# Three raw weight buffers against one converted one in a recurrence feeding two feed-forward layers

## The chip, the cores and the metric

The kernel runs on one core of one Trainium2 chip. The metric is the device time of one execution in microseconds; the median of three runs before the change is 770.36 us (769.48 to 771.55).

## The reference

Four batches of eight heads, 768 steps and a head size of 48 go through a gated linear recurrence; its output, 3072 tokens of 384, goes through two feed-forward layers (hidden sizes 2048 and 1024).

```python
for t in range(S):                                   # per batch and head, state is 48 x 48
    cur = einsum('bhd,bhe->bhde', u * kt, vt)
    y[:, :, t] = einsum('bhd,bhde->bhe', rt, state + cur)
    state = wt[..., None] * state + einsum('bhd,bhe->bhde', kt, vt)
...
h = x @ w_in;  x = (h - tanh(h)) @ w_out             # layer 1
...
h = x @ w_in2; e = exp(h - max(h)); h = h * e / (sum(e) + 1e-9)
x = (h - mean(h)) / sqrt(var(h) + 1e-6) * g_ln @ w_out2   # layer 2
```

The two pairs of weight matrices come as 64-bit floats, which the kernel reads as pairs of 32-bit words; all else is 32-bit.

## The kernel before, in words

**Units and blocks.** The recurrence is cut into 24 units of 128 steps (NU), all heads of a unit together. Four units give one block of 512 tokens (UB = 4, NB = 6 blocks). A unit goes through `att_pre` and `att_0` to `att_4`: transposes of w, r and k, a cumulative product of w by a scan (line 285), its logarithm and exponential on ScalarE (288, 289), products with r and k, score matmuls (312), a masked copy (314), transposes of k (318) that ScalarE copies to `kn` (319), the state update (328 to 340), and the output matmuls (354), which leave the tokens in `xs`. Units 0 to 7 (below TURN = 8) are loaded by `att_load` and transposed by TensorE; later ones by `load_turned` and VectorE.

**Layer 1.** A loop over s runs 96 steps, 16 a block. Step s does `part1` (nine matmuls into `hp`, line 401; a polynomial for h - tanh(h) with scratch tiles t, q and y; a split of the result into a rounded part and a rest, g) and `part2` of two steps before (nine matmuls into three accumulators `x2p`, line 425). At a block's end ScalarE copies the accumulators to `x2o` tiles (line 430), which borrow the tags q, t and y, and SyncE stores them (431). In the first and the last block (`ends`) the polynomial's middle term goes into `hp`, elsewhere into q.

**Weights.** Each of the 16 slices of layer 1's weights is loaded as raw 64-bit words into a tile `raw` (pool cvr, lines 364 to 387: four DMAs of 96 KB and one of 384 KB), converted by `convert` and written to the resident tile `wa`. The conversion is one ScalarE operation on the low words (121), three VectorE operations on each half (129, 130, 131, the last into `cv_x` of pool cv), a rounding copy on ScalarE (134) and a subtraction on GpSimd (135) that reads `cv_x` again. Both pools have two buffers. Slices 0 and 1 are loaded early; slice s+2 is loaded and converted in step s of the first block. Layer 2's eight slices are converted the same way in the last block (`conv_b`, into `wb`), with one pass over the whole tile and a scale (133).

**Flags.** Everything the fast path assumes is collected in a column per test of the tile `flags`: w within bounds for each unit (`check_w`, line 241: two ScalarE Relu passes, each followed by a read of the accumulator), the size of h, and the smallness of the weights' values (`check_pair`, lines 140 and 141, which re-loads a raw pair in the blocks after the first). For units 0 to 7 `check_w` stands in `att_pre` ahead of GpSimd's product (254), and its junk output goes to a q tile, or to the tile that 254 writes next.

**Order.** SyncE's queue issues all loads and stores in one order and waits at an instruction whose buffer is not free. The framework orders each engine's instructions ahead of time by priority (the order of the program's lines) and by its own estimate of when operands are ready; each engine then runs its list in order. Layer 2 (lines 463 to 568) follows the loop.

The lines the prediction speaks of, in short:

```python
cv = pool(L, "cv", 2); cvr = pool(L, "cvr", 2)              # 603, 604
v.tensor_tensor(x[:, s], a, L_[:, s], ALU.add)              # 131
nc.scalar.copy(hi, xf)                                      # 134
nc.gpsimd.tensor_tensor(lo, xf, hi, ALU.subtract)           # 135
q = self.gp.tile([128, BLK], F32, tag="q", name="q")        # 403
```

Of the kernel before, what the change touches and what calls it, by code (L numbers as in the profile page):

```python
# [8 lines left out]
F32 = mybir.dt.float32  # L9
F32R = mybir.dt.float32r  # L10
U32 = mybir.dt.uint32
I32 = mybir.dt.int32
U8 = mybir.dt.uint8
# [19 lines left out]
ROW = 4 * 4 * D  # L33
TURN = 2 * UB


W_LO, W_HI = 0.75, 1.34

# [20 lines left out]
class Kern:  # L59
# [7 lines left out]
    def setup(self, const):  # L67
        nc = self.nc
        self.ident = const.tile([128, 128], F32, name="ident")
        self.zeros = const.tile([128, 1], F32, name="zeros")  # L70
        self.ub = const.tile([128, H, D], F32, name="ub")
        self.mask = const.tile([128, 4, 128], U8, name="mask")
        self.cst = const.tile([128, 8], F32, name="cst")
        self.nflag = 2 * NU + NB * NM + NM + NM2
        self.flags = const.tile([128, self.nflag], F32, name="flags")
        make_identity(nc, self.ident)
        nc.vector.memset(self.zeros, 0.0)
        for i, val in enumerate((F_SB, -F_T2, W_LO, -W_HI, -0.5, P_SB, P_MIN, FLAG_MIN2)):
            nc.vector.memset(self.cst[:, i:i + 1], val)
        (self.c_fsb, self.c_t2, self.c_lo, self.c_hi, self.c_mhalf, self.c_sb, self.c_min,  # L80
         self.c_flag) = (self.cst[:, i:i + 1] for i in range(8))

    def setup_mask(self, ones):
        nc = self.nc
        nc.gpsimd.memset(ones, 1.0)
        nc.gpsimd.affine_select(
            out=ones, in_=ones, compare_op=ALU.is_gt, fill=0.0, base=0,
            pattern=[[0, 4], [1, 128]], channel_multiplier=-1,
        )
        nc.vector.tensor_copy(self.mask, ones)  # L90

# [20 lines left out]
    def convert(self, pool, raw, hi, lo, scale=None, bank=None):  # L112
# [10 lines left out]
        for i in range(n):  # L123
            s = slice(i * 2 * DM // n, (i + 1) * 2 * DM // n)
            if bank is None:
                a = x
            else:
                a = bank.tile([128, 4, C], F32, tag="a", name="cv_a").rearrange("p j t -> p (j t)")[:, 0:DM].bitcast(U32)
            v.tensor_scalar(a, H_[:, s], 3, 0x3FFFFFF8, ALU.logical_shift_left, ALU.bitwise_and)
            v.scalar_tensor_tensor(a, H_[:, s], 0xC0000000, a, ALU.bitwise_and, ALU.bitwise_or)  # L130
            v.tensor_tensor(x[:, s], a, L_[:, s], ALU.add)  # L131
        if scale is not None:
# [10 lines left out]
    def check_pair(self, rpool, n):  # L143

        raw = self.load_pair(rpool, n)
        with self.tc.issue_after(self.last_act.ins):
            self.check(raw, 2 * NU + NB * NM + n)

# [90 lines left out]
    def check_w(self, u, w, tmp):  # L239
        for i, (b, s) in enumerate(((self.c_lo, -1.0), (self.c_hi, 1.0))):  # L240
            self.nc.scalar.activation(tmp, w, AF.Relu, bias=b, scale=s,
                                      accum_out=self.flags[:, 2 * u + i:2 * u + i + 1])

    def att_pre(self, u):
        nc = self.nc
        t = self.rk(u)
        r, k = (t[:, 0, :, 0:D], t[:, 1, :, 0:D]) if u < TURN else (self.nat[:, 0], self.nat[:, 1])
        ruk = self.ruk
        if u <= UB:
            ruk = self.gp.tile([128, BLK], F32, tag="y", name="ruk")[:, 0:DM].rearrange("p (h d) -> p h d", h=H)  # L250
        if u < TURN:
            w = self.gp.tile([128, BLK], F32, tag="q", name="cw")[:, 0:DM].rearrange("p (h d) -> p h d", h=H) if u < UB else ruk
            self.check_w(u, t[:, 2, :, 0:D], w)
        nc.gpsimd.tensor_tensor(ruk, r, self.ub, ALU.mult)
        nc.gpsimd.tensor_tensor(ruk, k, ruk, ALU.mult)
        nc.vector.reduce_sum(self.dg[u % 2].rearrange("p e j -> p j e"), ruk.rearrange("p (j e) d -> p j e d", e=2), axis=AX)
# [44 lines left out]
    def att_2(self, u):  # L301
# [11 lines left out]
        for e in range(2):  # L313
            v.copy_predicated(self.aq[:, e], self.mask, ps[e])
        if u % NC < NC - 1:
# [79 lines left out]
    def part1(self, i, m):  # L395
# [6 lines left out]
        t = self.gp.tile([128, BLK], F32, tag="t", name="t")  # L402
        q = self.gp.tile([128, BLK], F32, tag="q", name="q")
        y = self.gp.tile([128, BLK], F32, tag="y", name="y")
# [5 lines left out]
        nc.scalar.activation(p, t, AF.Square, bias=self.c_fsb, scale=F_S)  # L410
        col = 2 * NU + i * NM + m
        self.last_dve = v.scalar_tensor_tensor(y, p, F_E, y, ALU.add, ALU.mult)  # L412
# [8 lines left out]
    def part2(self, i, m, gs):  # L421
# [5 lines left out]
        if m == NM - 1:  # L427
            for d in range(KM):
                o = self.gp.tile([128, BLK], F32, tag="qty"[d], name="x2o")
                self.nc.scalar.activation(o, self.x2p[d], AF.Copy, scale=-1.0)  # L430
# [162 lines left out]
def fast_path(tc, K, const):  # L593
# [8 lines left out]
    L, R, R2 = ExitStack(), ExitStack(), ExitStack()  # L602
    cv = pool(L, "cv", 2)
    cvr = pool(L, "cvr", 2)
    K.gp = pool(L, "gp", 2)
# [33 lines left out]
    for s in range(-2, NB * NM + 2):  # L639
# [37 lines left out]
        n, due = divmod(3 * (s - NM), 7)  # L677
        if 0 <= n < NM + NM2 and due < 3:
            K.check_pair(cvr, n)
# [219 lines left out]
```

## Time and profile before

| what | value |
|---|---|
| median of 3 runs | 770.36 us (769.48 to 771.55) |
| the profiled execution's own time | 775.22 us |
| its span in the trace | 773.4 us |
| busy in the span: PE, DVE, ACT, POOL | 725.0, 585.2, 490.8, 419.0 us |
| mean granted TensorE clock | 0.982 of full speed |
| DMA: moved, mean rate, share of 16 engines | 110.80 MB, 143 GB/s, 52.9% |

PE is TensorE, DVE VectorE, ACT ScalarE, POOL GpSimd, SPq the queue of SyncE that issues the transfers. Lines are numbered as in the kernel above. An engine runs its instructions in order, so a wait at one of them holds up all that stand behind it; a row of waits gives the total, the number and the longest.

### The profile page before, as it was taken

The numbers are of one execution on the slowest core, as the hardware profiler recorded it, in microseconds if no ns is written. First come the engines' busy times: TensorE is split into PE (matmuls) and PEld (weight loads), VectorE is DVE, ScalarE is ACT, GpSimd is POOL, SyncE is SP. The second block draws the span as 40 slices with busy tenths as digits, with TensorE's granted clock in tenths as the row PEclk, the third lists the DMA queues.
The fourth block names the chain that finished last, engine by engine and source line by source line (L and its number), as shares of the span: only waits on it lengthen the run. The fifth ranks groups of instructions, "written<-read, shape, count | busy, mean of one in ns | idle before, by whom it ended". The sixth has DMA issues, their size and how long they took to land.

```text
span 773.4 us, 13992 instructions
## 1 busy us (share of the span) xinstructions
PE 725.0 (94%) x4882; PEld 599.2 (77%) x4882; DVE 585.2 (76%) x999; ACT 490.8 (63%) x920; POOL 419.0 (54%) x397
## 2 busy tenths in 40 slices
PE   6558988999999999999999999999989999999986
PEld 4446667778877888887888887878769989989976
DVE  4868888877766687677677774487669999999992
ACT  4436777588676877686768665787745555554552
POOL 7424575666566666556655654467525454454440
PEclk9879999999999999999999999999999999999999
DMA  9962666666756756576555510232045555555631
GB/s 156 189 127 69 157 185 151 147 169 179 175 146 162 196 143 174 133 205 177 138 154 168 155 62 11 82 123 83 10 158 183 168 178 172 175 169 168 188 104 46
DMA packets 171632, 110.80 MB, mean 143 GB/s; under 512 B 93600, under 2 KB 160288, under 8 KB 171552
## 3 DMA queue, kind: packets, MB, share of 16 engines
q1 hardware_dynamic: 171552, 109.82, 52.9%
q8 instruction: 40, 0.66, 0.4%
q14 instruction: 40, 0.33, 0.1%
HBM read 88.81 MB, written 20.97 MB: 142 GB/s over the span
## 4 chain that ended last, share of the span: by engine, by line
PE 49%; DVE 28%; ACT 10%; DMA 5%; SPq 4%; issue 3%; POOL 1%; ACTq 0%; DVEq 0%; POOLq 0%
PE hp L401 19%; PE x2p L425 19%; DVE tw L539 6%; DVE so L514 4%; PE y L354 4%; DVE e L508 4%; DMA raw<-in_moe_w_out_dram 3%; ACT e L515 3%; DVE part L504 3%; PE qk L312 3%; SPq L367 2%; PE o L564 2%; DVE cv_x L131 2%; SPq L201 1%; PE kt L318 1%
## 5 line engine op out<-in xcount | busy, mean ns | idle before, releaser
L425 PE MATMUL x2p<-g,wa 128*128 128x512 f32 x864 | 226.0, 400 | 9.6 <-ACT g L415 7.9
L401 PE MATMUL hp<-xs,wa 128*128 128x512 f32 x864 | 216.0, 395 | 2.5 <-POOL wa L135 1.3
L425 PEld LDWEIGHTS x2p<-g,wa 128*128 128x128 f32 x864 | 158.7, 189 | 49.6 <-ACT g L415 9.9
L401 PEld LDWEIGHTS hp<-xs,wa 128*128 128x128 f32 x864 | 163.4, 190 | 39.7 <-POOL wa L135 2.3
L418 POOL TENSOR_TENSOR g<-y,g 128x512 fp32r<-128x512 f32 x96 | 129.6, 1351 | 48.4 <-ACT g L415 39.0
L407 DVE TENSOR_TENSOR y<-hp,t 128x512 f32<-128x512 f32 x96 | 65.8, 686 | 76.8 <-ACT t L406 60.4
L564 PE MATMUL o<-wb,ts 128*128 128x384 f32 x576 | 105.1, 336 | 2.5 <-POOL ts L543 2.5
L482 PE MATMUL h<-wb,x2s 128*128 128x512 f32 x432 | 104.1, 392 | 3.2 <-POOL x2s L471 1.7
L413 ACT ACTIVATE q<-t,cst 128x512 f32<-128x512 f32 x96 | 69.5, 724 | 55.7 <-DVE y L412 55.1
L564 PEld LDWEIGHTS o<-wb,ts 128*128 128x128 f32 x576 | 100.7, 188 | 4.8 <-POOL ts L543 3.2
L482 PEld LDWEIGHTS h<-wb,x2s 128*128 128x128 f32 x432 | 80.4, 188 | 20.7 <-POOL x2s L471 2.7
L417 POOL TENSOR_SCALAR g<-y 128x512 fp32r<-128x512 f32 x64 | 40.3, 630 | 81.5 <-DVE y L412 77.4
L406 ACT ACTIVATE t<-hp 128x512 f32<-128x512 f32 x96 | 56.5, 588 | 27.2 <-PE hp L401 26.3
L515 ACT ACTIVATE e<-so 128x1024 f32<-128x1024 f32 x24 | 25.5, 1061 | 59.6 <-DVE so L514 59.6
L543 POOL TENSOR_TENSOR ts<-tw,ts 128x512 fp32r<-128x512 f32 x44 | 55.9, 1292 | 4.4 <-ACT ts L542 4.4
L412 DVE SCALAR_TENSOR_TENSOR y<-q,y 128x512 f32<-128x512 f32 x64 | 51.4, 803 | 2.9
L471 POOL TENSOR_TENSOR x2s<-x2s 128x384 fp32r<-128x384 f32 x24 | 24.4, 1017 | 48.1 <-ACT x2s L470 43.7
L297 POOL TENSOR_TENSOR inv<-inc,kh 112x512 f32<-112x512 f32 x24 | 29.1, 1213 | 37.4 <-ACT kh L289 33.7
L410 ACT ACTIVATE q<-t,cst 128x512 f32<-128x512 f32 x64 | 46.3, 723 | 1.3
L539 DVE STREAM_TRANSPOSE tw<-sw 128x1024 f32<-128x1024 f32 x22 | 44.5, 2022 | 0.4 <-issue 0.3
L517 POOL TENSOR_TENSOR st<-st,cst 128x1 f32<-128x1 f32 x23 | 12.6, 549 | 53.0 <-DVE st L498 45.3
L121 ACT ACTIVATE raw<-raw 128x768 uint32<-128x768 uint32 x24 | 21.8, 908 | 27.9 <-DMA raw<-in_moe_w_out_dram 24.3
(138 smaller groups left out, 1182.4 us busy)
## 6 DMA issues: line engine op xcount, KB each, us to landing
raw<-in_moe_w_out_dram SPq DMA_DIRECT2D x48, 384.0 KB, 4.0
raw<-in_moe_w_in_dram SPq DMA_DIRECT2D x128, 96.0 KB, 2.8
dso<-so SPq DMA_DIRECT2D x22, 512.0 KB, 3.0
sw<-dso SPq DMA_DIRECT2D x88, 128.0 KB, 3.0
rkw<-in_k_dram SPq DMA_DIRECT2D x64, 96.0 KB, 2.7
rkw<-in_r_dram SPq DMA_DIRECT2D x64, 96.0 KB, 2.4
rkw<-in_w_dram SPq DMA_DIRECT2D x64, 96.0 KB, 2.4
raw<-in_moe_w_in_dram SPq DMA_DIRECT2D x16, 384.0 KB, 3.2
```

The costliest lines, as they stand in the source:

```text
L401: self.mm(hp, self.wa[:, a, m, j * 128:(j + 1) * 128], xs[:, b, j], start=n == 0, stop=n == len(seq) - 1)
L406: nc.scalar.activation(t, hp, AF.Square)
L407: v.tensor_tensor(y, hp, t, ALU.mult)
L412: self.last_dve = v.scalar_tensor_tensor(y, p, F_E, y, ALU.add, ALU.mult)
L413: self.last_act = nc.scalar.activation(q, t, AF.Relu, bias=self.c_t2, accum_out=self.flags[:, col:col + 1])
L418: g.tensor_tensor(gs[:, 1], y, gs[:, 0], ALU.subtract)
L425: self.mm(self.x2p[d], self.wa[:, a, m, sl], gs[:, b], start=m == 0 and n == 0, stop=m == NM - 1 and n == 2)
L482: self.mm(p[:, f], xs[:, a, j], w, start=q == 0, stop=q == 8)
L515: nc.scalar.activation(e, so, AF.Square, accum_out=va)
L539: self.turned = nc.vector.transpose(x.rearrange("p k (t b) -> p b k t", b=4), sw)
L543: nc.gpsimd.tensor_tensor(ts[:, 1, k], x[:, k], ts[:, 0, k], ALU.subtract)
L564: self.mm(p, ts[:, a, k], self.wb[:, b, k, DM:], start=q == 0, stop=q == 3 * NM2 - 1)
```

## The change

`cvr`, the pool of raw words, gets three buffers and `cv`, the pool of converted words, one. For layer 2 the last VectorE step of the conversion writes over the raw high words (every second word of the tile), which ScalarE and GpSimd then read; for layer 1 it still writes `cv_x`. The q tag gets one buffer. The mask becomes one 128x128 tile broadcast over four heads. The bounds of w are tested by one Square of (w - 1.045) and one Relu of its excess over 0.087025, with one accumulator read in place of two. For units 0 to 7 `check_w` goes out of `att_pre`; in its stead two more turns of `check_pair` (n = 24 and 25, in steps 72 and 75, the fifth block) re-load the w of four units each into a raw tile by four DMAs and test the 128x1536 values in two passes.

```diff
-        self.mask = const.tile([128, 4, 128], U8, name="mask")
+        self.mask = const.tile([128, 128], U8, name="mask")
...
-        nc.vector.tensor_copy(self.mask, ones)
+        nc.vector.tensor_copy(self.mask, ones[:, 0])
...
-            v.tensor_tensor(x[:, s], a, L_[:, s], ALU.add)
+            v.tensor_tensor(H_ if bank is None else x[:, s], a, L_[:, s], ALU.add)
+        if bank is None:
+            xf = H_.bitcast(F32)
...
-        raw = self.load_pair(rpool, n)
+        if n < NM + NM2:
+            raw = self.load_pair(rpool, n)
+            with self.tc.issue_after(self.last_act.ins):
+                self.check(raw, NW + NB * NM + n)
+            return
+        h = n - NM - NM2
+        raw = rpool.tile([128, 2, DM, 2], U32, tag="raw", name="raw").rearrange("p i f two -> p (i f two)").bitcast(F32)
+        w = raw.rearrange("p (i h d) -> p i h d", i=UB, h=H)
+        for i in range(UB):
+            b, c = divmod(UB * h + i, NC)
+            self.nc.sync.dma_start(out=w[:, i], in_=self.w[b, :, c * C:(c + 1) * C, :].rearrange("h p d -> p h d"))
         with self.tc.issue_after(self.last_act.ins):
-            self.check(raw, 2 * NU + NB * NM + n)
+            self.nc.scalar.activation(raw, raw, AF.Square, bias=self.c_mid)
+            self.nc.scalar.activation(raw, raw, AF.Relu, bias=self.c_rad, accum_out=self.flags[:, h:h + 1])
...
-        for i, (b, s) in enumerate(((self.c_lo, -1.0), (self.c_hi, 1.0))):
-            self.nc.scalar.activation(tmp, w, AF.Relu, bias=b, scale=s,
-                                      accum_out=self.flags[:, 2 * u + i:2 * u + i + 1])
+        self.nc.scalar.activation(tmp, w, AF.Square, bias=self.c_mid)
+        self.nc.scalar.activation(tmp, tmp, AF.Relu, bias=self.c_rad, accum_out=self.flags[:, u + NW - NU:u + NW - NU + 1])
...
-        if u < TURN:
-            w = self.gp.tile([128, BLK], F32, tag="q", name="cw")[:, 0:DM].rearrange("p (h d) -> p h d", h=H) if u < UB else ruk
-            self.check_w(u, t[:, 2, :, 0:D], w)
...
-            v.copy_predicated(self.aq[:, e], self.mask, ps[e])
+            v.copy_predicated(self.aq[:, e], self.mask.unsqueeze(1).to_broadcast([128, 4, C]), ps[e])
...
-        q = self.gp.tile([128, BLK], F32, tag="q", name="q")
+        q = self.gp.tile([128, BLK], F32, tag="q", name="q", bufs=1)
...
-                o = self.gp.tile([128, BLK], F32, tag="qty"[d], name="x2o")
+                o = self.gp.tile([128, BLK], F32, tag="qty"[d], name="x2o", bufs=1 if d == 0 else 2)
...
-    cv = pool(L, "cv", 2)
-    cvr = pool(L, "cvr", 2)
+    cv = pool(L, "cv", 1)
+    cvr = pool(L, "cvr", 3)
...
-        if 0 <= n < NM + NM2 and due < 3:
+        if 0 <= n < NM + NM2 + TURN // UB and due < 3:
```

## Rows read from the trace of the kernel before

**Rows 1.** Busy time by stretch: PE, PEld, DVE, ACT, POOL, granted clock, DMA share, GB/s

```profile
26.00:56.00 30.00, 18.57 (x278) 14.91 (x278) 21.61 (x47) 11.89 (x20) 10.39 (x9) 0.72 0.83 152
56.00:150.00 94.00, 81.88 (x597) 63.38 (x597) 81.59 (x155) 63.93 (x118) 56.00 (x42) 0.95 0.57 143
150.00:470.00 320.00, 318.19 (x2426) 255.93 (x2428) 228.49 (x401) 231.44 (x463) 192.98 (x186) 1.00 0.58 155
```

**Rows 2.** Chain of waits, by line, in 56 to 150 us

```profile
by line: DMA raw<-in_moe_w_out_dram 20.5%; PE hp L401 13.2%; PE x2p L425 8.2%; SPq L367 8.1%; DVE st L340 6.3%; issue 5.0%; PE qk L312 3.9%; ACT g L415 3.1%; ACT raw L121 2.8%; POOL g L418 2.8%; DVE y L407 2.7%; DVE cv_a L129 2.7%; PE y L35
```

**Rows 3.** ScalarE's waits for raw words, 56 to 150 us: total, times, longest

```profile
ACT raw L121 <- DMA raw<-in_moe_w_out_dram: 12.3, 7, 3.4
ACT raw L121 <- DMA raw<-in_moe_w_in_dram: 2.7, 1, 2.7
```

**Rows 4.** SyncE's own queue, its longest waiter in 20 to 150 us

```profile
SPq L367 <- DVE cv_x L131: 41.7, 11, 10.1
```

**Rows 5.** Chain of waits in 18 to 66 us, four pieces: start, us, what

```profile
31.88 0.72 ACT ruk L241 x2
...
32.62 0.71 ACT ruk L241 x2
...
37.19 5.21 DMA raw<-in_moe_w_out_dram
...
43.38 0.43 ACT kn L319
```

**Rows 6.** Timeline of TensorE: transposes that kn copies; busy time in 37 to 43 us

```profile
35.90 1.01 PE L318 MATMUL x2p<-ident,kh 112*128 112x112 f32 x4
...
37.00:43.00 6.00, 0.00 (x0) 0.00 (x0) 2.46 (x5) 1.32 (x2) 4.13 (x4) 0.50 1.09 215
```

**Rows 7.** Timeline of ScalarE: first and last of the 13 rounding copies of slices 2 to 14

```profile
66.90 0.82 ACT L134 CAST wa<-cv_x 128x768 fp32r<-128x768 f32 x1
...
147.12 0.82 ACT L134 CAST wa<-cv_x 128x768 fp32r<-128x768 f32 x1
```

**Rows 8.** Timelines, two conversions from the first write of cv_x to its last read

```profile
78.50 0.54 DVE L131 CUSTOM_DVE_ANT_0 cv_x<-raw,cv_a 128x768 uint16<-128x768 uint16 x1
...
83.39 1.84 POOL L135 TENSOR_TENSOR wa<-cv_x,wa 128x768 fp32r<-128x768 f32 x1
...
115.75 0.54 DVE L131 CUSTOM_DVE_ANT_0 cv_x<-raw,cv_a 128x768 uint16<-128x768 uint16 x1
...
117.86 0.55 DVE L131 CUSTOM_DVE_ANT_0 cv_x<-raw,cv_a 128x768 uint16<-128x768 uint16 x1
...
120.21 0.82 ACT L134 CAST wa<-cv_x 128x768 fp32r<-128x768 f32 x1
...
121.11 1.86 POOL L135 TENSOR_TENSOR wa<-cv_x,wa 128x768 fp32r<-128x768 f32 x1 [0.98 <-ACT wa L134]
```

**Rows 9.** Timeline of ScalarE at the end of the fourth block; the store's time to landing

```profile
415.29 0.59 ACT L430 ACTIVATE x2o<-x2p 128x512 f32<-128x512 f32 x1
...
416.80 0.72 ACT L413 ACTIVATE q<-t,cst 128x512 f32<-128x512 f32 x1 [0.25 <-DVE y L412]
...
422.24 0.71 ACT L410 ACTIVATE q<-t,cst 128x512 f32<-128x512 f32 x1
...
423.48 0.72 ACT L410 ACTIVATE q<-t,cst 128x512 f32<-128x512 f32 x1
...
424.20 0.72 ACT L413 ACTIVATE q<-t,cst 128x512 f32<-128x512 f32 x1
...
x2d<-x2o SPq DMA_DIRECT2D x18, 256.0 KB, 2.4
```

**Rows 10.** Groups of the two kinds of tests, by shape; busy time in 440 to 480 us

```profile
L141 ACT ACTIVATE raw<-raw,cst 128x768 f32<-128x768 f32 x24 | 23.9, 994 | 0.3
...
L241 ACT ACTIVATE cw<-rkw,cst 128x384 f32<-128x384 f32 x8 | 4.9, 616 | 4.7 <-DMA rkw<-in_w_dram 4.6
...
440.00:480.00 40.00, 40.00 (x308) 32.12 (x307) 24.19 (x42) 24.04 (x48) 22.48 (x23) 1.00 0.18 53
```

**Rows 11.** Groups, by shape: GpSimd's subtraction for layer 2

```profile
L135 POOL TENSOR_TENSOR wb<-cv_x,wb 128x768 fp32r<-128x768 f32 x8 | 17.0, 2119 | 3.0 <-PE x2p L425 3.0
```

More of the change, by code (lines that the diff above doesn't have):

```diff
@@ L34 @@
 TURN = 2 * UB
-W_LO, W_HI = 0.75, 1.34
+NW = NU - TURN + TURN // UB
+W_MID, W_RAD2 = 1.045, 0.087025
 P_MIN = 1e-30
@@ L69, in setup @@
         self.ident = const.tile([128, 128], F32, name="ident")
-        self.zeros = const.tile([128, 1], F32, name="zeros")
         self.ub = const.tile([128, H, D], F32, name="ub")
-        self.mask = const.tile([128, 4, 128], U8, name="mask")
+        self.mask = const.tile([128, 128], U8, name="mask")
         self.cst = const.tile([128, 8], F32, name="cst")
-        self.nflag = 2 * NU + NB * NM + NM + NM2
-        self.flags = const.tile([128, self.nflag], F32, name="flags")
+        self.nflag = NW + NB * NM + NM + NM2
+        flags = const.tile([128, self.nflag + 1], F32, name="flags")
+        self.flags, self.zeros = flags[:, 0:self.nflag], flags[:, self.nflag:]
         make_identity(nc, self.ident)
         nc.vector.memset(self.zeros, 0.0)
-        for i, val in enumerate((F_SB, -F_T2, W_LO, -W_HI, -0.5, P_SB, P_MIN, FLAG_MIN2)):
+        for i, val in enumerate((F_SB, -F_T2, -W_MID, -W_RAD2, -0.5, P_SB, P_MIN, FLAG_MIN2)):
             nc.vector.memset(self.cst[:, i:i + 1], val)
-        (self.c_fsb, self.c_t2, self.c_lo, self.c_hi, self.c_mhalf, self.c_sb, self.c_min,
+        (self.c_fsb, self.c_t2, self.c_mid, self.c_rad, self.c_mhalf, self.c_sb, self.c_min,
          self.c_flag) = (self.cst[:, i:i + 1] for i in range(8))
@@ L410, in part1 @@
         nc.scalar.activation(p, t, AF.Square, bias=self.c_fsb, scale=F_S)
-        col = 2 * NU + i * NM + m
+        col = NW + i * NM + m
         self.last_dve = v.scalar_tensor_tensor(y, p, F_E, y, ALU.add, ALU.mult)
```

## The prediction

> **What bounds the kernel now.** I read the busy times by stretch first, to find where TensorE is not the bound. From 150 to 470 us it is: 318.19 of 320 us busy at clock 1.00 [rows 1]. Nothing this change does to another engine there can shorten the time, short of a new stall. The stretches with slack are 26 to 56 us (18.57 of 30 us busy, clock 0.72) and 56 to 150 us (81.88 of 94, clock 0.95) [rows 1]. Whatever these two lose, all later work starts earlier by as much, so the change is priced in them.
>
> Then the chain of waits. From 56 to 150 us its largest entry is not an engine: the transfers of raw weights hold 20.5% of 94 us, 19.3 us, and SyncE's issue of them another 8.1%, 7.6 us [rows 2]. Why are they late? The queue's own waits say: SyncE stood 41.7 us, in 11 waits, before a raw load because VectorE's line 131 had not yet given a raw buffer back [rows 4]; and ScalarE, which has the first operation on the words, sat idle 12.3 + 2.7 = 15.0 us for them [rows 3]. So in the first block two raw buffers are too few: a load starts when the last conversion is over, and the next conversion waits for it. The rounding copies of slices 2 to 14 start at 66.90 and 147.12 us, 12 spacings of 6.69 us [rows 7]; a step of the first block takes that long.
>
> The start differs. On its chain stand unit 4's test of w (0.72 + 0.71 us) and 5.21 us of slice 2's raw transfer, after which ScalarE gets to `kn` of unit 2 at 43.38 [rows 5]. Its transposes were over at 36.91 [rows 6]: it stood behind the raw operation in ScalarE's list. TensorE did nothing from 37 to 43 us [rows 6]. But there the DMA engines have no room: share 1.09, 215 GB/s [rows 6].
>
> **The change part by part.** (1) *Test of w out of the early units.* Each unit loses two passes and two accumulator reads. On the chain stands only unit 4's pair, 1.43 us [rows 5]; the rest ran beside other work. What is late next is the logarithm behind it, which needs a VectorE scan ending at almost the same time, so I take 0.5 of a possible 1.4 us. GpSimd's product of unit 4, which waited for the test's junk, now waits for its r transfer alone.
>
> (2) *Third raw buffer, at the start.* Slice 2's load needs no buffer back and can be issued ahead of the loads of units 4 and 5. If so, `kn` of unit 2 moves from 43.38 to about 37.4, right behind its transposes: 6.0 us at most [rows 5, 6]. If the queue keeps its order, nothing: the DMA engines are full, and an earlier raw load only pushes the units' loads back. No row decides between them; I take the middle, 3 us, and keep 0 and 6 as ends.
>
> (3) *Third raw buffer, in the first block.* Load m then waits for the conversion three before, about 6.7 us sooner than now, against waits of 3.4 us at most [rows 3]: ScalarE's 15.0 us of waiting go. What is late next is either VectorE or the single `cv_x`. VectorE is busy 81.59 of 94 us [rows 1], so 0.868 of a spacing, 5.8 us: that floor allows 12 x (6.69 - 5.8) = 10.7 us.
>
> (4) *One buffer of converted words.* This adds a wait: line 131 of the next slice must follow GpSimd's line 135 of this one. The loop from the first write to the last read takes 78.50 to 85.23, 6.73 us, in one conversion and 115.75 to 122.97, 7.22 us, in another [rows 8]: mean 6.98, longer than the spacing now. Of it 0.54 + 0.55 + 0.82 + 1.86 = 3.77 us is work [rows 8] and 3.2 us is queueing, in good part behind ScalarE's waits for raw words (VectorE ended at 118.41, the rounding copy began at 120.21 [rows 8]). Without those I take 1.2 us off the queueing, two thirds of that gap of 1.8, and 0.5 on for VectorE's wait for GpSimd's signal: 6.98 - 1.2 + 0.5 = 6.3 us, between the work alone (3.77) and 6.98 + 0.5 = 7.48, nearer the latter because its rows are the same loop. (3) and (4) together are then 12 x (6.69 - 6.3) = 4.7 us gained, with ends of 10.7 gained and 12 x (7.48 - 6.69) = 9.5 lost. Behind the new wait on VectorE stand the products of the polynomial (lines 407, 412); ScalarE and GpSimd wait for these, and then TensorE for g.
>
> (5) *One q buffer.* Inside a block each step writes q twice on ScalarE and the second write waits for VectorE already, so order costs nothing. At a block's end it does: now two line-410 writes follow each other (422.24, 423.48) before the first step's 413 (424.20) [rows 9], which needs two buffers, and the store's copy (415.29) stands ahead of a 413 (416.80) that uses the other one [rows 9]. With one buffer the copy goes behind that 413, the store takes 2.4 us to land [rows 9], about 418 + 0.6 + 2.4 = 421, just ahead of 422.24; then one line 410 waits some 1.5 us for the 413 before it. TensorE has matmuls in stock there. Four ends at 0 to 1.5 us each: I take 0.3, 1.2 us lost in all.
>
> (6) *Late tests and the rest.* The two new turns cost 4 DMAs each and two passes over 128x1536; from 994 ns for 768 values [rows 10] at most 4 x 2.0 = 8 us of ScalarE, in a stretch where it works 24.04 of 40 us, the DMA share is 0.18, and TensorE is full [rows 10]: 0; were that cover gone, 8 us. SyncE issues them behind raw loads whose buffers come free early, so no store waits for them. Units 8 to 23 lose one accumulator read each: 0. In layer 2 the subtraction now reads every second word; a nearest row is its 2119 ns [rows 11], and if it doubled, 8 x 2.1 = 17 us of GpSimd beside a full TensorE; I take 0, with 3 us as the end. The broadcast mask: 0.
>
> Sum: 0.5 + 3 + 4.7 - 1.2 = 7.0 us. The profiled execution took 775.22 us (span 773.4 and 1.8 around it), so 768.2; it lies 4.9 us above the median, and on the median the same 7.0 us give 763.4.
>
> **The rivals.** *A, both stretches open fully.* Conversions at VectorE's floor (10.7), `kn` unblocked (6.0), 1.4 of the test, no loss at the ends: 18 us, 752. Granted clock speaks for it: 0.72 and 0.95 [rows 1] are the 1.2 GHz level in parts, after TensorE stood idle; at 1.00 the 81.88 us of the first block would be 77.8, an estimate. Against it: VectorE would have to run without a gap.
>
> *B, no change.* The start is held by the DMA engines, (2) gives 0, and the loop of `cv_x` holds the first block at 6.6 us a slice: 0.5 + 0 + 1.1 - 1.2, 770. The share of 1.09 [rows 6] speaks for the first half; the 41.7 us of SyncE's waits for a buffer [rows 4] and the share of 0.57 after 56 us [rows 1] speak against it. The Trainium skill, Perfetto Trace Analysis, "What 'DMA-bound' means", counts saturated DMA engines as a bound of their own; by that rule (2) is 0. The trace agrees up to 43 us and not after.
>
> *C, slower.* VectorE waits at line 131 for GpSimd, whose line 135 stands behind g's split and the recurrence's products. The loop stays at its present 6.98 us and gets the 0.5 on top: 7.48 a slice, 9.5 us lost, less 3.5 of the start, plus 1.2: 777.6; with half of the loop's loss, 4.7, it is 772.8. It decides from a loop above 6.69 + 0.2 us. For it: the two measured loops are both above 6.69 [rows 8]. Against: a good part of their waiting is what the third raw buffer takes away. The Trainium skill, Trainium Kernel Development and Optimization, "Best Practices", says to double-buffer, which speaks against this part of the change and for the other.
>
> **How the numbers follow.** Forecast 0.48 (757 to 768 us), A 0.11, B 0.19, C 0.22. About 0.3%, 2.3 us, is what a measurement of this kernel can tell from no change. Faster 0.59, same 0.19, slower 0.22. The range reaches into A by a part and into C up to its middle and a little beyond: 755.5 to 774.5.
>
> **What would show it.** Right: ScalarE's waits for raw words in the first block fall from 15.0 to under 4 us, SyncE's waits for line 131 all but vanish, the rounding copies come every 6.2 to 6.4 us, and `kn` of unit 2 stands near 37 to 40 us. Wrong: VectorE shows a wait for GpSimd's line 135 of more than some 6 us in total (C); `kn` still at 43 (half of B); a gap of TensorE of over 1 us at each block's end (part 5); or the same gain in the first block given back behind 470 us, where layer 2's conversions now read strided words.

## The result, and the profile after

The changed kernel took 781.04 us (median of 4 runs, 779.90 to 783.63) against 770.95 for the kernel before (4 runs): a ratio of 1.0113, 95% interval 1.0083 to 1.0142. It is slower by about 9 us; forecast were 763.4, and 774.5 as the range's upper end. The profiled execution took 780.75 us with a span of 779.0, close to its median. That of before (775.22) is slower than each of its four runs, so the two traces lie 5.6 us apart where the medians lie 10.1 apart; a second trace of before (e9, below) has a span of 771.7.

Busy time by stretch in the changed kernel (columns as in [rows 1]):

```profile
26.00:56.00 30.00, 18.10 (x276) 14.95 (x276) 20.62 (x44) 10.96 (x16) 8.93 (x8) 0.70 0.89 170
37.00:43.00 6.00, 0.33 (x4) 0.11 (x2) 3.66 (x8) 0.83 (x1) 3.83 (x3) 0.80 0.95 200
56.00:150.00 94.00, 82.24 (x544) 62.34 (x538) 81.66 (x157) 58.05 (x102) 55.74 (x43) 0.95 0.57 141
150.00:470.00 320.00, 317.28 (x2452) 255.27 (x2452) 227.10 (x397) 230.18 (x446) 189.23 (x183) 0.99 0.60 158
```

The stretches with slack have not been filled. TensorE's busy time in 56 to 150 us, most of the first block, is 82.24 of 94 us, against 81.88 [rows 1], but the profile counts 544 matmuls in it, against 597: less is done in the same time. The waits tell a part of the reason. ScalarE's, in 56 to 150 us:

```profile
ACT raw L122 <- DMA raw<-in_moe_w_out_dram: 18.1, 8, 3.2
...
ACT raw L122 <- DMA rkw<-in_w_dram: 2.0, 1, 2.0
```

SyncE's queue in 20 to 150 us, and VectorE in 56 to 160 us:

```profile
SPq L377 <- DVE cv_x L132: 39.9, 12, 10.3
```

```profile
DVE cv_x L132 <- POOL wa L138: 1.0, 2, 0.8
```

The waits that the third raw buffer was to take away are all there: 20.1 us on ScalarE in place of 15.0 [rows 3], 39.9 on SyncE in place of 41.7 [rows 4]. And the wait that rival C feared, VectorE for GpSimd's line 138 (135 before), is 1.0 us in all. So neither side of the prediction's argument about the first block is what happened. The timeline of ScalarE shows what did (slice 3's rounding copy stands last):

```profile
68.39 0.82 ACT L137 CAST wa<-cv_x 128x768 fp32r<-128x768 f32 x1
69.11 0.69 ACT L420 ACTIVATE hp<-t,cst 128x512 f32<-128x512 f32 x1
69.74 0.47 ACT L369 CAST xs<-y 128x384 fp32r<-128x384 f32 x1
70.11 0.61 ACT L425 CAST g<-y 128x512 fp32r<-128x512 f32 x1
73.69 0.92 ACT L122 ACTIVATE raw<-raw 128x768 uint32<-128x768 uint32 x1 [2.98 <-DMA raw<-in_moe_w_out_dram]
74.51 0.62 ACT L425 CAST g<-y 128x512 fp32r<-128x512 f32 x1
75.50 0.60 ACT L416 ACTIVATE t<-hp 128x512 f32<-128x512 f32 x1 [0.37 <-PE hp L411]
76.13 0.84 ACT L137 CAST wa<-cv_x 128x768 fp32r<-128x768 f32 x1
```

The line 122 at 73.69 is the sixth of the kernel, slice 5's, and it stands ahead of the rounding copy of slice 3: two slices ahead. In the kernel before, the operation on raw words at the same place is slice 4's, one slice ahead of the copy below it, slice 3's:

```profile
72.60 0.92 ACT L121 ACTIVATE raw<-raw 128x768 uint32<-128x768 uint32 x1 [3.37 <-DMA raw<-in_moe_w_out_dram]
...
74.65 0.84 ACT L134 CAST wa<-cv_x 128x768 fp32r<-128x768 f32 x1
```

Counted over the whole first block, slices 4 to 15 stand two ahead after and mostly one ahead before. The framework writes each engine's list ahead of time; given a third buffer it put the operation one slice further up, and the transfer that it waits for is as late, relative to it, as before.

The chain of waits in 56 to 150 us has the same two entries as before, the transfers of raw words and SyncE's issue of them, 19.3% and 9.6% where it had 20.5% and 8.1% [rows 2]:

```profile
by line: DMA raw<-in_moe_w_out_dram 19.3%; SPq L377 9.6%; issue 8.4%; PE hp L411 8.1%; DMA rkw<-in_w_dram 7.2%; DVE st L350 6.6%; DVE cv_x L132 5.1%; DVE cv_a L130 4.3%; DVE cv_a L131 3.7%; DVE y L422 3.4%; ACT wa L137 3.2%; PE qk L322 2.4%
```

The start did not open either. On ScalarE the `kn` of unit 2 still stands behind the operation on slice 2's words:

```profile
43.22 0.88 ACT L122 ACTIVATE raw<-raw 128x768 uint32<-128x768 uint32 x1 [2.94 <-DMA raw<-in_moe_w_in_dram]
44.01 0.51 ACT L329 COPY kn<-x2p 128x448 f32<-128x448 f32 x1
```

while TensorE had ended its transposes long before, and waited:

```profile
36.72 0.60 PE L328 MATMUL x2p<-ident,kh 112*128 112x112 f32 x4
44.57 0.34 PE L338 MATMUL ds<-vt,kn 128*64 128x48 f32 x1 [7.24 <-ACT kn L329]
```

44.01 stands against 43.38 [rows 5]. SyncE's list explains it: the third buffer is free, yet the loads of units 4 and 5 still stand ahead of slice 2's, which is issued from 35.49 on.

```profile
30.47 0.88 SPq L215 DMA_DIRECT2D rkw<-in_w_dram  x1
...
32.60 1.05 SPq L215 DMA_DIRECT2D rkw<-in_k_dram  x1
35.49 1.92 SPq L377 DMA_DIRECT2D raw<-in_moe_w_in_dram  x4
```

### The profile page after: what moved, and what is told of

Same layout as the page of the kernel before. It is cut to its first block, busy times and chain, and to the rows that moved or that the text cites. A ratio compares the mean times of both kernels' runs of the same rounds, so it can differ in the third digit from the quotient of the medians.

```text
span 779.0 us, 13963 instructions
## 1 busy us (share of the span) xinstructions
PE 730.8 (94%) x4882; PEld 604.1 (78%) x4882; DVE 585.1 (75%) x999; ACT 484.6 (62%) x878; POOL 417.2 (54%) x397
## 4 chain that ended last, share of the span: by engine, by line
PE 50%; DVE 27%; ACT 8%; DMA 5%; SPq 4%; issue 3%; POOL 1%; ACTq 0%; DVEq 0%; POOLq 0%
PE hp L411 19%; PE x2p L435 18%; DVE tw L549 6%; DVE so L524 4%; PE y L364 4%; DVE e L518 4%; ACT e L525 3%; PE qk L322 3%; DVE part L514 3%; DMA raw<-in_moe_w_out_dram 3%; PE o L574 2%; SPq L377 2%; SPq L215 1%; DVE raw L132 1%; PE ds L338 1%
## 5 line engine op out<-in xcount | busy, mean ns | idle before, releaser
L435 PE MATMUL x2p<-g,wa 128*128 128x512 f32 x864 | 223.7, 399 | 9.2 <-ACT g L425 7.7
L411 PE MATMUL hp<-xs,wa 128*128 128x512 f32 x864 | 218.4, 398 | 3.9 <-POOL wa L138 3.3
L428 POOL TENSOR_TENSOR g<-y,g 128x512 fp32r<-128x512 f32 x96 | 127.5, 1328 | 51.9 <-ACT g L425 42.0
L492 PEld LDWEIGHTS h<-wb,x2s 128*128 128x128 f32 x432 | 80.4, 188 | 20.1 <-POOL x2s L481 2.3
L427 POOL TENSOR_SCALAR g<-y 128x512 fp32r<-128x512 f32 x64 | 39.9, 623 | 95.1 <-DVE y L422 87.2
L138 POOL TENSOR_TENSOR wa<-cv_x,wa 128x768 fp32r<-128x768 f32 x16 | 29.3, 1834 | 23.7 <-ACT wa L137 21.4
```

Of the source, the lines that this page charges most:

```text
L411: self.mm(hp, self.wa[:, a, m, j * 128:(j + 1) * 128], xs[:, b, j], start=n == 0, stop=n == len(seq) - 1)
L428: g.tensor_tensor(gs[:, 1], y, gs[:, 0], ALU.subtract)
L435: self.mm(self.x2p[d], self.wa[:, a, m, sl], gs[:, b], start=m == 0 and n == 0, stop=m == NM - 1 and n == 2)
L492: self.mm(p[:, f], xs[:, a, j], w, start=q == 0, stop=q == 8)
```

## The experiments

Ratios are to the kernel before on the same chip in the same session: 773.31 us there for e1 to e4, 773.10 for e5 to e8, 773.63 for e9 to e12. An offset of 0.001 is 0.8 us. The ratio is not the quotient of the two medians and differs from it by up to 0.0017 (for e10 the medians give 0.9952). Beside the ratio I use one mark of the profiled execution, the end of layer 1 (the last copies of the accumulators to `x2o`): 568.00 us in the first trace of before, 565.20 in its second, 572.60 in the changed kernel. The two traces of one kernel are 2.8 us apart at this mark, so a smaller difference between single traces says little. What lies behind that mark differs from kernel to kernel for a reason of its own (last section).

**First, the buffers one by one.** e1, one converted buffer alone, in the kernel before:

```diff
-    cv = pool(L, "cv", 2)
+    cv = pool(L, "cv", 1)
```

> The kernel before with one buffer of converted words in place of two, nothing else. If the single cv_x is the cost (rival C of the prediction, a loop of 7.5 us a slice), it is slower by 6 to 10 us: 777 to 781. If the loop hides behind the late raw words anyway, it stays within 2 us of 771, and the loss of the change lies in another part. In the trace I look at VectorE's waits at line 131 for GpSimd's line 135: over 6 us in total by the first, under 2 by the second.

Measured 783.60 us, ratio 1.0141 (1.0123 to 1.0160): as slow as the whole change and more. VectorE's waits for GpSimd in the first block, the mark of rival C, are 1.1 us. The traced execution took 776.69, the fastest of the six, and so shows only a part of the loss. It loses nothing in the first block: the rounding copies of layer 2's slices there begin 5.1 us earlier than in before's first trace and end 8.3 us later.

```profile
493.39 0.84 ACT L134 CAST wb<-cv_x 128x768 fp32r<-128x768 f32 x1
...
548.19 0.83 ACT L134 CAST wb<-cv_x 128x768 fp32r<-128x768 f32 x1
556.61 0.82 ACT L134 CAST wb<-cv_x 128x768 fp32r<-128x768 f32 x1
```

Before, for the first and the last of them:

```profile
498.45 0.84 ACT L134 CAST wb<-cv_x 128x768 fp32r<-128x768 f32 x1
...
548.36 0.83 ACT L134 CAST wb<-cv_x 128x768 fp32r<-128x768 f32 x1
```

So the single buffer seems to be dear in layer 2, where the change does not use it (it writes over the raw words there). e8, below, tests that.

e2, one q buffer alone (the three q and x2o lines of the change, and `bufs=1` for the junk tile `cw` of the tests of w):

```diff
...
-        q = self.gp.tile([128, BLK], F32, tag="q", name="q")
+        q = self.gp.tile([128, BLK], F32, tag="q", name="q", bufs=1)
...
```

> The kernel before with one q buffer, nothing else. If the block ends are the cost, ScalarE waits at each of the five ends for the store of x2o or for the step before, and the time rises by 3 to 8 us: 774 to 779. By the working of the prediction (0.3 us an end) it rises by 1.2 us, no more than can be told from no change: 770 to 773.

Measured 775.14 us, 1.0016 (0.9997 to 1.0035): 1.2 us, though the interval takes in no change at all.

e3, the changed kernel with two raw buffers:

```diff
-    cvr = pool(L, "cvr", 3)
+    cvr = pool(L, "cvr", 2)
```

> The changed kernel with the third raw buffer taken back (two), all else of the change kept. If the third buffer does what the prediction said, it is slower than the changed kernel's 781 by 5 us or more: 786. If the third buffer brings nothing, because ScalarE's list only puts its operation on the raw words one slice further ahead (in the changed kernel the operation on slice 5 stands before the rounding copy of slice 3, before it was the one on slice 4), it is at 779 to 783, and ScalarE's waits for raw words in 56 to 150 us are again 15 to 20 us.

Measured 778.96 us, 1.0073 (1.0056 to 1.0089). The third raw buffer does not help the change: with it 1.0113 (1.0083 to 1.0142), without it 1.0073, so that it costs some 3 us. ScalarE's waits at line 122 in the first block are 16.5 us without, 20.1 with it, and line 122 stands one slice ahead without, two with it.

e4, the changed kernel with all buffers as before (2 raw, 2 converted, 2 of q); what is left is the late tests, layer 2's words and the mask:

```diff
...
-    cv = pool(L, "cv", 1)
-    cvr = pool(L, "cvr", 3)
+    cv = pool(L, "cv", 2)
+    cvr = pool(L, "cvr", 2)
```

> The changed kernel with two buffers each of raw words, converted words and q, as before; the new test of w, its late turns, the one mask and the strided conversion of layer 2 kept. If the buffers are the whole loss, it comes out at 769 to 773, as before, or a little below for the tests that the first block no longer holds. If the late tests or the strided words cost, it stays at 776 or above.

Measured 775.94 us with a wide scatter (769.99 to 783.08, 10 runs), 1.0021 (0.9993 to 1.0048): 1.6 us, between the two forecasts and within the noise. Most of the loss is then in the buffers, or in the lists that are laid out for them.

**Then ScalarE's list.** In e5 and e6 a dependence of order alone is added, to the kernel before and to the changed kernel; no buffer, no transfer and no word of data changes:

```diff
-        nc.scalar.activation(L_, L_, AF.Copy, scale=2.0**-29)
+        with self.tc.issue_after(self.last_hi.ins) if bank is not None and self.last_hi is not None else nullcontext():
+            nc.scalar.activation(L_, L_, AF.Copy, scale=2.0**-29)
...
-        nc.scalar.copy(hi, xf)
+        self.last_hi = nc.scalar.copy(hi, xf)
```

> The kernel before, with one thing added: in the first block ScalarE's operation on the raw words of a slice (line 121) is queued behind the rounding copy of the slice before it, so that it no longer stands ahead of that copy in ScalarE's list. Theory S (ScalarE's fixed list is what the first block loses: an operation that waits for a transfer holds up the rounding copy, and with it GpSimd, behind it): ScalarE's waits for raw words in 56 to 150 us fall from 15.0 us to under 8, and the time is 2 to 4 us below the kernel before (ratio 0.995 to 0.997). Theory L (the buffers' loops set the pace, wherever the wait is shown): the waits may change, the time does not by more than 1 us (0.999 to 1.001), or it grows because the operation comes later.

> The changed kernel with the same thing added as in the run before (the operation on raw words queued behind the rounding copy of the slice before it). Theory S (the third raw buffer brought nothing because ScalarE's list spent it by putting the operation on raw words two slices ahead): the waits for raw words in 56 to 150 us fall from about 20 us to under 6, `kn` of unit 2 comes earlier than 44 us, and the time is 4 to 6 us below the changed kernel (ratio to before 1.003 to 1.007 where the changed kernel stands at 1.011). Theory L (the one converted buffer's loop sets the pace): no gain, 1.010 to 1.013.

e5 measured 767.67 us, 0.9919 (0.9889 to 0.9949); e6 770.94 us, 0.9959 (0.9941 to 0.9978). The changed kernel goes from 1.0113 to 0.9959, 12 us, by one added order between two operations of ScalarE. Both gains are larger than theory S said. e5's waits in 56 to 150 us:

```profile
ACT raw L123 <- DMA rkw<-in_w_dram: 1.4, 1, 1.4
ACT raw L123 <- DMA raw<-in_moe_w_out_dram: 1.3, 2, 0.8
```

2.7 us in place of before's 15.0 [rows 3]; in e6 there are none. One part of S was wrong: `kn` of unit 2 stays at 45.1 us in e6. The operation on slice 2's words, at 44.31, still stands ahead of it there, so e6 does not test the list at the start.

e7, the changed kernel with layer 1 too converted over the raw words, so that no `cv_x` is used in the first block:

```diff
-            v.tensor_tensor(H_ if bank is None else x[:, s], a, L_[:, s], ALU.add)
-        if bank is None:
-            xf = H_.bitcast(F32)
+            v.tensor_tensor(H_[:, s], a, L_[:, s], ALU.add)
+        xf = H_.bitcast(F32)
```

> The changed kernel in which layer 1's conversion too writes over the raw high words, so that nothing uses cv_x in the first block and the loop from its first write to its last read is gone; a raw buffer is instead held until the subtraction is over, and the rounding copy and the subtraction read every second word. Theory L (the loop of the one converted buffer is the loss): VectorE never waits for GpSimd there, 3 to 5 us below the changed kernel (ratio to before 1.004 to 1.007). Theory S (ScalarE's list): waits for raw words stay at 15 us or more, and the time stays within 1.5 us of the changed kernel (1.009 to 1.013).

Measured 774.90 us, 1.0030 (1.0006 to 1.0054), just below theory L's bounds and outside those of S. But it does not prove L: the list moved here as well (line 122 now stands one ahead for most slices and two for three of them) and the waits at it fell to 8.1 us. Inconclusive by itself.

e8, e1 with layer 2 converted over the raw words, as in the change, so that the single `cv_x` is left in the first block only:

```diff
-    cv = pool(L, "cv", 2)
+    cv = pool(L, "cv", 1)
...
-            v.tensor_tensor(x[:, s], a, L_[:, s], ALU.add)
+            v.tensor_tensor(H_ if bank is None else x[:, s], a, L_[:, s], ALU.add)
+        if bank is None:
+            xf = H_.bitcast(F32)
```

> The kernel before with one converted buffer as in e1, and in layer 2 alone the conversion over the raw high words, as the change has it, so that only the first block is left with a single cv_x. Theory L (the single buffer costs in the first block): as slow as e1, ratio 1.010 to 1.015. Theory T (e1's loss came in the last block, where layer 2's conversions shared the one buffer, as its trace says): ratio 0.995 to 1.002, and the rounding copies of layer 2 within 2 us of the kernel before.

Measured 773.41 us, 1.0000 (0.9978 to 1.0021). One converted buffer costs nothing that can be told from the noise in the first block of this kernel, and e1's loss was layer 2's: the two kernels differ in layer 2's conversion alone, and their lists for the first block are the same. Theory L falls here. ScalarE still waits 14.7 us for raw words in e8; the kernels below, in which it does not, put VectorE's waits for GpSimd at 0.7 us or less.

**Then the size of the step.** e9 is the kernel before again.

> The kernel before once more, for a second trace of it. The first trace took 775.22 us against a median of 770.36, and 12 spacings of its rounding copies were 6.69 us each, while e2, with the same list of ScalarE, had 6.32. If that stretch differs from run to run with the list unchanged, this trace has a spacing between 6.3 and 6.7 and the same order of line 121 and line 134; the time stays at a ratio of 0.997 to 1.003.

Measured 774.26 us, 1.0001 (0.9977 to 1.0025). The list is the same, and the 12 spacings of the rounding copies are (144.44 - 68.66) / 12 = 6.32 us where the first trace had 6.69 [rows 7]:

```profile
68.66 0.82 ACT L134 CAST wa<-cv_x 128x768 fp32r<-128x768 f32 x1
...
144.44 0.82 ACT L134 CAST wa<-cv_x 128x768 fp32r<-128x768 f32 x1
```

So the prediction's base was the slower of two traces of the same kernel; ScalarE's waits for raw words were 11.0 us here.

e10, the changed kernel with line 122 behind the rounding copy of the slice two before (`last_hi` becomes a list, and its last but one entry is waited for), so that it stands one ahead, as in the kernel before:

```diff
...
+        with self.tc.issue_after(self.last_hi[-2].ins) if bank is not None and self.last_hi[-2] is not None else nullcontext():
```

> The changed kernel with line 122 of a slice queued behind the rounding copy of the slice two before it, so that it stands one slice ahead, as in the kernel before, and not two (the changed kernel) or none (e6). Theory S (the place in ScalarE's list is what counts, and each place ahead costs): waits for raw words in 56 to 150 us of 8 to 16 us, a ratio between e6 and the changed kernel, 1.001 to 1.007. Rival P (any added order between the two operations helps, by shifting other work): as fast as e6, 0.994 to 0.998. Rival L (the single converted buffer): 1.009 to 1.013.

Measured 769.95 us, 0.9969 (0.9946 to 0.9991): outside the bounds of S as I had put it, inside those of P. S had forecast 8 to 16 us of waits, because it counted places and not buffers; that reading came after the run. With three buffers, one place ahead leaves a buffer over, and the waits for raw words go:

```profile
ACT raw L124 <- DMA raw<-in_moe_w_out_dram: 1.7, 2, 1.0
```

and the rounding copies of slices 2 and 14 stand (141.00 - 67.64) / 12 = 6.11 us apart:

```profile
67.64 0.82 ACT L139 CAST wa<-cv_x 128x768 fp32r<-128x768 f32 x1
...
141.00 0.83 ACT L139 CAST wa<-cv_x 128x768 fp32r<-128x768 f32 x1 [0.24 <-DVE cv_x L134]
```

In the changed kernel, whose slice 2 stands above at 68.39, that is (148.75 - 68.39) / 12 = 6.70:

```profile
148.75 0.84 ACT L137 CAST wa<-cv_x 128x768 fp32r<-128x768 f32 x1 [0.25 <-DVE cv_x L132]
```

On e10's chain of waits in 56 to 150 us the transfers of raw words have 3.2%, where the changed kernel has 19.3%:

```profile
by line: PE hp L413 14.5%; issue 9.8%; DVE cv_a L132 6.9%; DVE st L352 6.5%; POOL wa L140 5.8%; DVE cv_x L134 5.0%; PE x2p L437 4.9%; DVE cv_a L133 4.7%; DVE y L424 4.1%; PE qk L324 3.6%; DMA raw<-in_moe_w_out_dram 3.2%; DVE y L419 3.0%; DM
```

P, that any added order would do, has this against it: the same dependence on the copy three before confirms the place that line 122 has in the changed kernel, and then all five engines' lists come out as they were (read from the lists; that kernel was not run). It is the move that counts, not the dependence. The other half of P, that the shifts in the other engines' lists help, is not ruled out by it.

e11, e4 (all buffers as before) with the dependence of e5; and e12, e6 with two raw buffers:

> The changed kernel with the buffers of before (two raw, two converted, two of q) and the operation on raw words queued behind the rounding copy of the slice before it, as in e5 and e6: against e5 it differs by the late tests, the strided words of layer 2 and the mask. If these cost nothing in the time, as e4 says (1.002, interval 0.999 to 1.005), the ratio is that of e5 to within the start's loss of 1 to 1.5 us: 0.992 to 0.995. If the buffers are harmless once the list is mended and the tests are what is left of e6's distance to e5, it is 0.995 to 0.997.

> e6 with two raw buffers in place of three: what the third one is worth when ScalarE's list doesn't spend it. Theory S: with the operation queued behind the rounding copy, ScalarE asks for the words of a slice one conversion later, so a load has that time ahead even with two buffers, and the third is worth little: within 0.002 of e6 (0.994 to 0.998), in the first block waits for raw words under 4 us. Rival (the third buffer does what it was thought to do once the list allows it): 2 to 5 us slower than e6, 0.998 to 1.003.

e11 measured 768.59 us, 0.9935 (0.9915 to 0.9955): late tests, strided words and mask cost 0.0016 against e5, 1.2 us, which is within the noise. e12 measured 773.31 us, 0.9990 (0.9973 to 1.0007). That is the rival's number, 2.4 us behind e6, while the waits, 3.0 us, are as S forecast. In the traces e12 stands at 565.29 at the end of layer 1 and e6 at 564.33, 1 us of their 3.3, and the rest is behind that mark; but the mark's own scatter is larger than that, so where the 2.4 us lie is open.

All kernels together; "ahead" is how many slices the operation on raw words stands ahead of the rounding copies in ScalarE's list, "waits" its whole idle time at that operation in 56 to 150 us, "spacing" that of the rounding copies of slices 2 to 14:

| kernel | raw buffers | ahead | waits, us | spacing, us | end of layer 1 | ratio |
|---|---|---|---|---|---|---|
| before, two traces | 2 | 1 | 15.8, 11.5 | 6.69, 6.32 | 568.0, 565.2 | 1 |
| e1 | 2 | 1 | 11.9 | 6.49 | 566.0 | 1.0141 |
| e2 | 2 | 1 | 11.9 | 6.32 | 566.3 | 1.0016 |
| e8 | 2 | 1 | 14.7 | 6.63 | 567.9 | 1.0000 |
| e4 | 2 | 1 | 13.7 | 6.54 | 571.0 | 1.0021 |
| e3 | 2 | 1 | 16.5 | 6.64 | 572.8 | 1.0073 |
| after | 3 | 2 | 20.1 | 6.70 | 572.6 | 1.0113 |
| e7 | 3 | 1 to 2 | 8.1 | 6.64 | 569.3 | 1.0030 |
| e5 | 2 | 0 | 2.7 | 6.19 | 563.4 | 0.9919 |
| e11 | 2 | 0 | 2.3 | 6.15 | 563.4 | 0.9935 |
| e12 | 2 | 0 | 3.0 | 6.23 | 565.3 | 0.9990 |
| e10 | 3 | 1 | 3.1 | 6.11 | 562.4 | 0.9969 |
| e6 | 3 | 0 | 0.0 | 6.06 | 564.3 | 0.9959 |

Take "ahead" and one off the number of buffers: where nothing is left (the first seven lines), ScalarE waits 11 to 20 us; where one or two are left, about 3 us or less. That is the table's one rule, and it holds in every line but e7, where the list is mixed and a raw buffer is held longer. The spacing follows: 6.32 us and more in the first seven, 6.06 to 6.23 in the last five. The gap of 0.09 us a slice between the two groups is smaller than what before's two traces differ by, but it holds in all of these twelve kernels. Among the kernels without a buffer left the waits order the end of layer 1 only roughly: e3 and after wait longest and are last, but e4 is near them with 13.7 us.

Put together by pairs, the ratios also say what the dependence and the third raw buffer are each worth, to within 2 to 3 us:

| what is added | to which kernel | worth, us |
|---|---|---|
| dependence, none ahead | before (e5) | -6.3 |
| the same | e4 (e11) | -6.6 |
| the same | e3 (e12) | -6.4 |
| the same | after (e6) | -11.9 |
| third raw buffer | e3 (after) | +3.1 |
| third raw buffer | e12 (e6) | -2.4 |

So the third buffer costs where ScalarE's list is free to spend it, and gains where it isn't. But of the 8.7 us by which the change is slower, only those 3.1 came with it. The other 5.6 are there with two raw buffers (e3), and nearly the same with the dependence in both kernels (e12 against e5, 0.0071, 5.5 us). Of these, one q buffer (e2, 1.2) and the tests, words and mask (e4, 1.6) make 2.8; for the other 2.8 no single run accounts, and the errors of the runs add up to about as much. e12's 0.0055 behind e11 is the same open point.

Nor does the spacing hold all that the changed kernel loses. At the rounding copy of slice 14 it is 1.6 and 4.3 us behind the two traces of before, at the end of layer 1 4.6 and 7.4: some 3 us come after that copy. e3, e4 and e12 lose as much there or a little more, e10 0.5. From the changed kernel to e10, 7.0 of the 10.2 us at the end of layer 1 lie in the twelve spacings.

What stays open: the added order moved other engines' lists too, since the framework lays them all out together; no run moves ScalarE's place alone. Counted in the lists, e10 differs from the changed kernel by 41 operations of ScalarE's, 72 of VectorE's and 7 of GpSimd's. A shift of that size need not change the time by itself: e8 differs from the kernel before by 75 operations of VectorE's, and its ratio is 1.0000. That the cause is the order of the lists, and not the buffers, the transfers or the work, e10 shows against the changed kernel. That it is ScalarE's wait among them rests on five kernels in which waits, spacing and, but for e12, the end of layer 1 went below both traces of before together, and on the chain.

The fastest kernel is e5: the kernel before with one dependence added, 0.8% faster than it and about 1.9% faster than the change.

## Why the prediction was wrong

**The step that failed** is part (3): "Load m then waits for the conversion three before, about 6.7 us sooner than now [...]: ScalarE's 15.0 us of waiting go." It took the order of ScalarE's list as given and gave the new buffer to the transfer. The list isn't given: it is laid out again for each kernel, and here it spent the buffer on an earlier place for the waiting operation. e10 shows the counterfactual: with the list held at the place it had before, ScalarE's waits at the operation are 3.1 us, where they are 20.1 in the changed kernel and 15.8 and 11.5 in the traces of before; the spacing is 6.11, and the change is 0.9969, faster. From e10 to the changed kernel, 1.0113 - 0.9969 = 0.0144, 11 us, is the price of the lists' order. In the traces 10.2 of them (572.60 - 562.36) lie ahead of the end of layer 1. The reading of [rows 4] that led there fails too. SyncE's waits before a raw load were to "all but vanish"; in e10, where ScalarE's waits for raw words are nearly gone, they are still there, and so they do not show that a buffer is short:

```profile
SPq L379 <- DVE cv_x L134: 37.5, 12, 10.3
```

**Parts (3) and (4) together, with the list held,** came out near their size, in part by luck. Forecast were 6.3 us a slice; e10 has 6.11, between the forecast and VectorE's floor of 5.8. The forecast gain of 4.7 us took 6.69 as the base; the mean of before's two traces is 6.5, and 12 x (6.5 - 6.11) = 4.7; by the first trace alone it is 7.0, by the second 2.5. And e5, with no third buffer, has 6.19, so most of this gain comes with the list and not with the buffer. The 0.5 us a slice for VectorE's wait for GpSimd came from no row; what VectorE waited was 1.0 us in all.

**Rival C** named the right sign and the wrong mechanism. Its mark, over 6 us of VectorE waiting for GpSimd, stands at 1.0 us, and e8 finds no cost of the single buffer in the first block (1.0000, 0.9978 to 1.0021). That its 777.6 lies nearest to what was measured is chance.

**Part (2), the start,** was given 3 us of a possible 6 and brought none: the queue kept its order, which the prediction had as its lower end and as half of rival B. The DMA share there, in 37 to 43 us, is 0.95, where it was 1.09 [rows 6], so that an earlier load would have found little room; no run issued it earlier. This is the Trainium skill's point in Perfetto Trace Analysis, "What 'DMA-bound' means", that saturated DMA engines are a bound of their own: the shares of 1.09 and 0.95 at the start agree with it.

**Part (1)** was given 0.5 us; ScalarE is busy 6.66 us in 0 to 26 where it was 12.21, and nothing came earlier for it: the first operation on raw words, held by a transfer for 5.25 us, starts at 27.91, where it started at 26.53 in the kernel before. So 0.

**Part (5)**, 1.2 us lost to one q buffer, fits e2's 1.2, whose interval is -0.2 to 2.7. But the store does not land ahead of the next write to q, as the part had it: in the changed kernel ScalarE waits for it, 1.7 us at each of the first two block ends (160 to 345 us).

```profile
ACT q L420 <- DMA x2d<-x2o: 3.4, 2, 1.7
```

**Part (6)** was taken as 0 with ends of 8 and 3 us; e4 (1.6) and e11 against e5 (1.2) put it at a little over 1 us, neither clear of the noise.

The ledger with the list held is then -4.7 + 1.2 + 1.2 = -2.3 us, and e10 measured 0.0031 of 773.6 = -2.4. So close a fit is luck: each term is uncertain by 2 us or so, and the medians alone give -3.7. The forecast's other 4.7 us were 3.5 of the start and 1.2 of part (6). Between -2.4 and +8.7 stands the order of the lists alone.

On the page named for double-buffering (the Trainium skill, Trainium Kernel Development and Optimization, "Best Practices"), which the prediction set against part (4): the page speaks of overlapping DMA with compute, and the converted words pass from engine to engine. No run here bears it out for the converted words of layer 1 (e8), and e1 does for those of layer 2, 10.9 us.

## What to carry to other kernels

In this kernel an added buffer bought time only where the instruction that waits for it kept its place. Count, in the list of the engine that runs it, how many items ahead of its consumer it stands, and compare that with the number of buffers less one, before and after. Where a framework lays the lists out, pin the waiting instruction behind the work that it would hold up; here one such dependence, without any buffer, was worth 6.3 us (e5), and the third raw buffer 2.4 with the dependence in place (e6 against e12). And trace the kernel before twice when a forecast rests on the length of one of its steps: 6.69 and 6.32 us were the same list.

## What the runs showed of the hardware

From the end of layer 1 to the end of the span the kernels took 203.0 us (e5, e11) to 207.3 (e12), and 205.4 and 206.5 in the two traces of before; e1, where words of layer 2 come late, is left out. One VectorE operation differs with it: the centring of the 128x1024 tile `so`. Its group in 575 to 745 us in e11, and then in e12:

```profile
L526 DVE TENSOR_SCALAR so<-e,st 128x1024 f32<-128x1024 f32 x21 | 24.3, 1159 | 0.8
```

```profile
L526 DVE TENSOR_SCALAR so<-e,st 128x1024 f32<-128x1024 f32 x21 | 32.8, 1560 | 0.7
```

A single one is 0.75 us long where it runs fast, and up to 1.9 us elsewhere. In e11's 591.89 it begins 0.13 us before GpSimd's pair of subtractions of line 555 ends (589.47 + 2.55); in e12's 651.92 it begins with 1.24 us of that pair still to come. e11:

```profile
591.89 0.75 DVE L526 TENSOR_SCALAR so<-e,st 128x1024 f32<-128x1024 f32 x1
```

```profile
589.47 2.55 POOL L555 TENSOR_TENSOR ts<-tw,ts 128x512 fp32r<-128x512 f32 x2
```

e12:

```profile
651.92 1.78 DVE L526 TENSOR_SCALAR so<-e,st 128x1024 f32<-128x1024 f32 x1
```

```profile
650.61 2.55 POOL L555 TENSOR_TENSOR ts<-tw,ts 128x512 fp32r<-128x512 f32 x2
```

The longer time is the short one plus most of what GpSimd had left: 1.78 is 0.75 + 1.03, and 1.24 us of the pair were to come. The Trainium skill, SBUF — State Buffer, "SBUF: two separate sides", says that VectorE and GpSimd share a pair of ports as an exclusive lock, held for a whole instruction while the other engine is blocked; on VectorE's side it names operations in a mode with two ports, or with two inputs in SBUF. The times agree with it; that this operation runs in such a mode no run here shows.

The operation is fast 3 times in before, after and e12, 7 times in e5 and e11, and then grows long. The kernel before and e5 have the same layer 2, and e5 passes through this stretch 2.4 and 3.5 us faster than the two traces of before. So a part of e5's gain lies there: at the end of layer 1 it is 1.8 to 4.6 us ahead of the two traces of before, at the end of the span 5.3 to 7.0. That the longer operation is the whole of this is not shown: e7, whose operation is long from the fourth on, took 203.7 us. Nor is it shown what sets how many are fast. The changed kernel lost nothing there: its 206.4 us for that stretch are those of before.
